# A spectral mixer ahead of routed experts: batch 1 through DRAM, batch 2's stores put off, nested conditions at the end

## The chip, the cores and the metric

The kernel runs on one core of one Trainium2 chip. The metric is the time of one execution on the device in microseconds, as the median of several runs. The core has five engines that run their own instruction streams in order and wait for each other through semaphores: TensorE (PE, with its weight load PEld), VectorE (DVE), ScalarE (ACT), GpSimd (POOL) and SyncE (SP). SP, ACT and POOL also issue DMAs; all DMAs share 16 DMA engines.

## The reference, cut to what matters

```python
# x: (8, 2496, 256); filt_r, filt_i: (1249, 256)
X = np.fft.rfft(x, axis=1)
y = np.fft.irfft(X * (filt_r + 1j * filt_i)[None], n=2496, axis=1)   # (8, 2496, 256)

x = y.reshape(19968, 256)
expert_idx = token_ids * np.int64(2654435761) % np.int64(8)
for e in range(8):
    mask = expert_idx == e
    h = np.maximum(x[mask] @ w1[e], 0.0)         # w1[e]: (256, 1024)
    out[mask] = h @ w2[e]                        # w2[e]: (1024, 256)
```

Each of the 8 batches is filtered along its 2496 positions by a Fourier transform. Then each of the 19968 rows goes through the two-layer network of the one expert that its token number names.

## The kernel before, in words

**The transform.** 2496 = 39 x 64, so a transform has three stages. Stage 1 multiplies by the 39-point table `wf_t`. Stage 2 multiplies by the 64-point table `d_t` (`forward`, PSUM tile `pb`), applies the filter on VectorE (four products and a sum, tiles `y` and `z`), and multiplies by `e_t` (`back`, tile `pc`). Stage 3 multiplies by `wi_t` (tile `pd`) and scatters the finished rows into the DRAM tensor `xs`, each row at the place that its expert gives it (`scatter`, an indirect DMA on GpSimd, 22 for each batch). Stage 1 and stage 3 of a batch come as 6 groups u = 0 to 5 (`NU`), stage 2 as 10 pairs of frequencies (`NS // 2`).

**Two ways between the stages.** Batches 2 to 7 go through DRAM. `stage1` writes rows into the buffer `t1`, which is stored to the DRAM tile `d1` (three parts v = 0 to 2, four DMAs). `load2` reads `d1` back in another order, as five groups g of four frequencies (tile `t2`, two DMAs each). `back` stores its result to `d2`, and `load4` reads that for stage 3 (tile `t`, parts v). Batches 0 and 1 stay on the chip: `stage1_c` writes columns into `mixed`, `turn2` transposes them on TensorE (tile `pt`), `back_c` and `turn4` do the same on the way to stage 3. The buffers `t1`, `t2`, `g`, `mixed` and `out` of the batches are all parts of one tile `mid` of ten slots, or of the space of the expert weights `wts`; `slots` says which.

**The experts.** Rows are taken in tiles of 128 that belong to one expert each. `load` fetches the rows of a pair of tiles (`xg`; the first four loads in `begin`, half of them on ScalarE's queue), `numbers` copies their row numbers (`no`), `turn` transposes a tile (`xt`), `up` does the first layer (32 matmuls, `ups`), `down` the second (16 matmuls, `dps`) and scatters the result into the output. `weights` loads an expert's weights where the expert changes. Tiles come in four groups (`STAGES`): the first 30 tiles hold rows of batches 0 and 1 alone, so they can run while later batches are still transformed. 159 tiles (`NSURE`) are always there; up to four more depend on the token numbers, and each of three conditions (`tc.If`) runs one, one or two of them.

**The order of the work** is written out by hand: the list `todo` holds pairs of a time and a piece of work and is sorted. Pieces with a negative time come ahead of the first tile. A time from 0 on is counted in tiles: a piece at 5.0 to 5.5 stands ahead of tile 5's up, one at 5.5 to 6.0 between its up and its down. `spaced(t0, t1, n)` spreads n pieces evenly. `chain(k)` interleaves `turn2` of step k + 1, `back_c` of step k - 2 and `forward` of step k over batches 0 and 1, so steps 10 to 19 belong to batch 1. `part1`, `part2` and `part3` are stages 1 to 3 of the later batches with their loads. Each engine and each queue carries out its instructions in this order, so a wait holds up all that stands behind it on the same engine.

Of the kernel before, what the change touches and what calls it, by code (L numbers as in the profile page):

```python
# [20 lines left out]
B, S, C = 8, 2496, 256  # L21
# [8 lines left out]
NS, NQ = N1 // 2 + 1, 64  # L30
# [3 lines left out]
NK = 2 * H * NS  # L34
SG = 4
XG = 4
NU = (HN + XG) // XG
# [6 lines left out]
NT = (N + E * (TB - 1)) // TB  # L44
# [8 lines left out]
NSURE = NT - 4  # L53
# [66 lines left out]
def kernel(  # L120
# [10 lines left out]
    nc = tc.nc  # L131
# [9 lines left out]
    def pool(stack, name, bufs, space=None):  # L141
# [28 lines left out]
    mid = cpool.tile([P, 10, SG * C], F32)  # L170
    wts = cpool.tile([P, 4, DP * F], F32)
    held = wts[:].rearrange("p k f -> p (k f)")
    slots = {"t1": [mid[0:NK, k:k + 2, :].rearrange("p k (j c) -> p (k j) c", c=C) for k in (5, 7)],
             "t2": [mid[:, k, :].rearrange("p (s c) -> p s c", c=C) for k in range(4)],
             "g": [mid[:, k, :].rearrange("p (s c) -> p s c", c=C) for k in (9, 4)]}

    def slot(kind):
        slots[kind].append(slots[kind].pop(0))
        return slots[kind][-1]

    class Batch:


        def __init__(self, b):
            self.b = b
            self.d1 = self.d2 = None
            self.x, self.t2, self.t4, self.p = {}, {}, {}, {}
            self.g = None
            if b < 2:

                own = mid[:, 5 * b:5 * b + 5, :].rearrange("p k f -> p (k f)")
                self.mixed = own.rearrange("p (h n s) -> p h n s", h=2, s=NS)
                after = (held[:, 0:NS * C] if b == 0 else mid[:, 0:5, :].rearrange("p k f -> p (k f)"))
                self.out = after.rearrange("p (h n s) -> p h n s", h=2, s=NS)

        def load1(self, v):
# [42 lines left out]
        def stage1(self, u):  # L239
            if self.d1 is None:  # L240
                self.d1 = dpool.tile([N2, 2 * NS, C], F32, name=f"d1_{self.b}", tag="d1")
            v, half = divmod(u, XL // XG)
            sl = slice(half * XG, half * XG + XG)
            if half == 0:
                self.t1 = slot("t1")
            self.products(wf_t, (NR, NR), 2 * NS, self.x[v][:, sl, :], self.t1[:, sl, :], nc.scalar.copy, u, "pa")
            if half == 1:


                eng = nc.scalar if self.b == 2 else nc.gpsimd  # L250
                for dram, chip in self.parts(self.d1, self.t1, v):
                    eng.dma_start(out=dram, in_=chip)

        def load2(self, g):
            t2 = slot("t2")
            for p in range(2):
                a0 = p * NS + SG * g
                nc.sync.dma_start(out=t2[p:P:2, :, :],
                                  in_=self.d1[:, a0:a0 + SG, :])
            self.t2[g] = t2  # L260

        def forward(self, u):
            ps = fps.tile([P, 2, C], F32, name=f"pb_{self.b}_{u}", tag="f")
            for i in range(2):
                s = 2 * u + i
                rhs = self.t2[u][:, i, :] if self.b < 2 else self.t2[s // SG][:, s % SG, :]
                nc.tensor.matmul(out=ps[:, i, :], lhsT=d_t[:, s, :], rhs=rhs, start=True, stop=True)  # L267

            sl = slice(2 * u, 2 * u + 2)
            y, z = [ppool.tile([P, 2, C], F32, name=f"{n}_{self.b}_{u}", tag="p") for n in "yz"]
            nc.vector.tensor_tensor(out=y[:], in0=ps[:], in1=f_t[0][:, sl, :], op=OP.mult)  # L273
            for k in range(2):
                a, b = slice(64 * k, 64 * k + 64), slice(64 - 64 * k, 128 - 64 * k)
                nc.vector.tensor_tensor(out=z[b], in0=ps[a], in1=f_t[1][a, sl, :], op=OP.mult)  # L276
            nc.vector.tensor_tensor(out=y[:], in0=y[:], in1=z[:], op=OP.add)  # L277
            self.p[u] = y
# [119 lines left out]
    def weights(i, which):  # L398

        if i >= NT:  # L400
            return
        if i >= 2 and which == 0:
            ws[i] = ws[i - 2][0:2]
        eng, kw = nc.sync, {}
        if which == 0:
            ws[i].append(eng.value_load(chunk_i[0:1, 0, i:i + 1], min_val=0, max_val=E - 1))
            if i >= 2:
                ws[i].append(eng.value_load(chunk_i[0:1, 1, i:i + 1], min_val=0, max_val=1))
        e = ws[i][2]
        if i >= 2:  # L410
            kw = {"cond": ws[i][3]}
        if which == 0:


            for f in (slice(0, F // 2), slice(F // 2, F)) if i < 2 else (slice(0, F),):
                eng.dma_start(out=ws[i][0][:, :, f],
                              in_=moe_w1[bass.ds(e, 1)].rearrange("one (p dp) f -> p (one dp) f", p=P)[:, :, f], **kw)
        else:
            eng.dma_start(out=ws[i][1], in_=moe_w2[bass.ds(e, 1)].rearrange("one (fp p) d -> p (one fp) d", p=P), **kw)
# [234 lines left out]
    def spaced(t0, t1, n):  # L654
        return [t0 + (t1 - t0) * u / n for u in range(n)]

    def part1(b, at, loads=None):
        bt = batches[b]
        if loads is None:

            loads = [at[2 * v] - 2.5 * (at[1] - at[0]) for v in range(NV)]
        return ([(at[u], lambda u=u: bt.stage1(u)) for u in range(NU)] +
                [(loads[v], lambda v=v: bt.load1(v)) for v in range(NV) if b > 0])

    def part2(b, at, ready):
        if isinstance(ready, list):
            bt = batches[b]
            return ([(at[u], lambda u=u: bt.stage2(u)) for u in range(NS // 2 + 1)] +
                    [(t, lambda g=g: bt.load2(g)) for g, t in enumerate(ready)])
        bt = batches[b]  # L670
        return ([(at[u], lambda u=u: bt.stage2(u)) for u in range(NS // 2 + 1)] +
                [(max(at[2 * g] - 4.5 * (at[1] - at[0]), ready), lambda g=g: bt.load2(g)) for g in range(NS // SG)])

    def part3(b, at, ready=None):
        bt = batches[b]
        if b < 2:
            return [(at[u], lambda u=u: bt.stage3(u)) for u in range(NU)]
        return ([(at[u], lambda u=u: bt.stage3(u)) for u in range(NU)] +
                [(max(at[2 * v] - 2.5 * (at[1] - at[0]), ready), lambda v=v: bt.load4(v)) for v in range(NV)])
# [5 lines left out]

    def chain(k):

        for step, j in ((Batch.turn2, k + 1), (Batch.back_c, k - 2), (Batch.forward, k)):
            if 0 <= j < NS:
                step(batches[j // (NS // 2)], j % (NS // 2))  # L690


# [6 lines left out]
    todo += [(t, lambda k=k: way_back(k)) for k, t in enumerate((-150.44, -146.5, -141.8, -137.5, -133.8))]  # L699
    todo += [(-150.4, lambda: first.turn2(0))]  # L700
    todo += [(t, lambda k=k: chain(k)) for k, t in enumerate(spaced(-150, -105, NS + 2))]
    todo += [(t, lambda u=u: second.stage1_c(u)) for u, t in enumerate(spaced(-147.5, -132, NU))]
    for bt, at in ((first, spaced(-123.7, -105, NU)), (second, spaced(-103, -85, NU))):
        todo += [(t - 2.6, lambda bt=bt, u=u: bt.turn4(u)) for u, t in enumerate(at)]
        todo += [(t, lambda bt=bt, u=u: bt.stage3(u)) for u, t in enumerate(at)]
    todo += [(-135, lambda: nc.sync.dma_start(out=wi_t[:], in_=wi_dram.ap()))]
    todo += part1(2, spaced(-102, -87, NU), [-119, -117.5, -116])
    todo += [(t, lambda k=k: weights(k // 2, k % 2)) for k, t in enumerate((-99, -98.9, -98.8, -98.7))]
    todo += [(-76, lambda: begin())]

    todo += part1(3, spaced(1.5, 6.5, NU), [-74.6, -74.5, 2.5]) + part1(4, spaced(15, 20.5, NU))
    todo += part1(5, spaced(21, 27, NU)) + part1(6, spaced(36, 46, NU)) + part1(7, spaced(50, 60, NU))
    todo += part2(2, [-74] + spaced(.55, 5.5, N_2 - 1), [-78, -75, -74.9, -74.8, 1.2]) + part2(3, spaced(9.2, 15.7, N_2), 6.6)
    todo += part2(4, spaced(22, 31, N_2), 20.5) + part2(5, spaced(31.2, 46, N_2), 28)
    todo += part2(6, spaced(48, 62, N_2), 47) + part2(7, spaced(63.2, 80, N_2), 61)
    todo += part3(2, spaced(7, 14, NU), 5.6) + part3(3, spaced(17, 25, NU), 15.6)
    todo += part3(4, spaced(33, 44, NU), 31.5) + part3(5, spaced(49, 63, NU), 46.5)
    todo += part3(6, spaced(67, 83, NU), 62) + part3(7, spaced(84, 101, NU), 81)
    todo.sort(key=lambda t: t[0])
# [95 lines left out]
    used = []  # L815
# [23 lines left out]
    spare = mid[:, 0, :].rearrange("p (i d t) -> p i d t", i=NT - NSURE, d=DP)  # L839
    for i in range(NSURE, NT):  # L840
        turn(i, spare[:, i - NSURE])
    for some in (range(NSURE, NSURE + 1), range(NSURE + 1, NSURE + 2), range(NSURE + 2, NT)):
        with tc.If(used[0] > some[0]):
            for i in some:
                ht = work.tile([P, FP, TB], F32, name=f"ht_{i}", tag="ht")
                numbers(i)
                up(i, ht)
                weights(i + 2, 0)
                down(i, ht)
                weights(i + 2, 1)  # L850


# [1 line left out]
_INS = ['x', 'filt_r', 'filt_i', 'moe_token_ids', 'moe_w1', 'moe_w2']  # L854
# [24 lines left out]
```

## Time and profile before

| what | value |
|---|---|
| median of 9 runs | 1520.94 us (1517.33 to 1523.45) |
| the profiled execution's own time | 1523.25 us |
| its span, first to last instruction | 1521.4 us |
| mean granted TensorE clock | 0.983 |
| PE, PEld busy | 1456.7 us (96%), 1341.1 us (88%) |
| DVE, ACT, POOL busy | 534.5, 234.0, 499.1 us |
| chain that ended last | PE 88%, DMA 8%, issue 1%, DVE 1% |
| DMA | 226.06 MB, mean 149 GB/s |

In a line of the timeline stand the start in us, the duration in us, the engine, the line of the kernel, the operation, what it writes and reads, and in square brackets how long the engine had been idle and what ended that. SPq, ACTq and POOLq are the queues of these engines: the instructions that issue DMAs, wait, or branch. In a line of the chain stand the start, the duration, and the work or the DMA that took that time. In a line of stretches stand the stretch, its length, the busy time of PE, PEld, DVE, ACT and POOL (with the number of instructions), the granted TensorE clock, the busy share of the DMA engines, and GB/s.

### The profile page before, as it was taken

How to read it: one execution, taken by the hardware profiler on the slowest of the kernel's cores; microseconds unless marked ns; L12 is line 12 of the kernel's file. 1: busy time of each engine (PE TensorE's matmuls, PEld its weight loads, DVE VectorE, ACT ScalarE, POOL GpSimd, SP SyncE). 2: the span in 40 equal slices, each digit the busy share in tenths (PEclk: the TensorE clock that was granted, in tenths of full speed). 3: DMA queues.
4: the chain of work that ended last, by engine and by line, in shares of the span. 5: the costliest groups of instructions: out<-in, count | busy, mean ns of one | idle time of the engine just before them, and what ended most of it. 6: DMA issues, size and time to landing. Idle time of an engine off the chain costs nothing.

```text
span 1521.4 us, 25837 instructions
## 1 busy us (share of the span) xinstructions
PE 1456.7 (96%) x9340; PEld 1341.1 (88%) x9340; DVE 534.5 (35%) x1008; ACT 234.0 (15%) x401; POOL 499.1 (33%) x802
## 2 busy tenths in 40 slices
PE   6995998998999999999999999999999999999996
PEld 6984897897989999989999999899999999999995
DVE  5962533632344443244434442222222221222221
ACT  3652120121121111111111110000000000000000
POOL 6565123544432343224432433233212111211111
PEclk9998999999999999999999999999999999999998
DMA  8267757669855963755657533653422423232320
GB/s 214 69 200 208 237 158 180 210 188 249 255 183 163 256 181 93 226 168 164 193 133 199 177 120 98 176 153 97 134 60 61 129 87 97 52 108 62 92 88 25
DMA packets 186988, 226.06 MB, mean 149 GB/s; under 512 B 101653, under 2 KB 157389, under 8 KB 180890
## 3 DMA queue, kind: packets, MB, share of 16 engines
q1 hardware_dynamic: 154615, 146.92, 35.3%
q0 software_dynamic: 28096, 73.51, 15.0%
q10 hardware_dynamic: 4147, 3.94, 0.9%
q8 instruction: 76, 1.25, 0.3%
q14 instruction: 54, 0.44, 0.1%
HBM read 415.94 MB, written 75.08 MB: 323 GB/s over the span
## 4 chain that ended last, share of the span: by engine, by line
PE 88%; DMA 8%; issue 1%; DVE 1%; POOL 0%; SPq 0%; ACT 0%; ACTq 0%; POOLq 0%; DVEq 0%
PE ups L790 36%; PE dps L802 34%; PE pd L226 5%; PE pb L267 4%; PE pc L289 3%; PE pa L226 3%; DMA t<-d 1%; DMA wts<-in_moe_w_dram 1%; DMA wts<-in_x_dram 1%; DMA d<-mid 1%; PE pc L339 1%; DMA mid<-d 1%; DMA d_t<-d_tbl 1%; PE pu L354 1%; DMA x<-in_x_dram 1%
## 5 line engine op out<-in xcount | busy, mean ns | idle before, releaser
L790 PEld LDWEIGHTS ups<-xt,wts 128*128 128x128 f32 x5088 | 597.4, 193 | 15.9 <-issue 7.5
L790 PE MATMUL ups<-xt,wts 128*128 128x128 f32 x5088 | 598.6, 277 | 4.8 <-issue 3.3
L802 PE MATMUL dps<-wts,ht 128*128 128x256 f32 x2544 | 575.7, 380 | 0.0
L802 PEld LDWEIGHTS dps<-wts,ht 128*128 128x128 f32 x2544 | 475.5, 191 | 60.4 <-ACT mid L292 0.8
L806 POOL DMA_INDIRECT out_dram<-osb,no x159 | 158.3, 995 | 571.4 <-DVE osb L805 456.8
L796 DVE TENSOR_SCALAR ht<-ups 128x512 f32<-128x512 f32 x159 | 110.0, 692 | 490.2 <-PE ups L790 484.1
L794 ACT ACTIVATE ht<-ups 128x512 f32<-128x512 f32 x159 | 94.9, 597 | 880.3 <-PE ups L790 835.0
L385 POOL DMA_INDIRECT xs<-o,sidx x176 | 178.0, 1011 | 109.5 <-issue 43.3
L805 DVE COPY osb<-dps 128x256 f32<-128x256 f32 x159 | 67.5, 425 | 362.3 <-PE dps L802 360.8
L773 POOL COPY no<-xg 32x2 int32<-32x2 int32 (+1 forms) x328 | 60.2, 184 | 262.3 <-DMA out_dram<-osb,no 180.6
L276 DVE TENSOR_TENSOR z<-pb,filt 64x512 f32<-64x512 f32 x160 | 110.1, 688 | 2.3
L226 PE MATMUL pd<-t,wi_t 120*117 120x256 f32 x320 | 79.8, 394 | 10.4 <-DMA t<-d 10.0
L267 PE MATMUL pb<-mid,d_t 128*128 128x256 f32 x240 | 63.9, 390 | 19.2 <-DMA mid<-d 19.2
L226 PEld LDWEIGHTS pd<-t,wi_t 120*117 120x117 f32 x320 | 58.8, 188 | 23.3 <-DMA t<-d 6.3
L273 DVE TENSOR_TENSOR y<-pb,filt 128x512 f32<-128x512 f32 x80 | 54.3, 679 | 61.6 <-PE pb L267 61.3
L292 ACT COPY mid<-pc 128x512 f32<-128x512 f32 x60 | 35.1, 585 | 230.4 <-PE pc L289 230.4
L780 DVE STREAM_TRANSPOSE xt<-xg 128x256 f32<-128x256 f32 x159 | 69.1, 434 | 0.0
L267 PEld LDWEIGHTS pb<-mid,d_t 128*128 128x128 f32 x240 | 44.4, 195 | 25.5 <-issue 16.6
L289 PE MATMUL pc<-y,e_t 128*128 128x256 f32 x240 | 61.7, 380 | 0.0
L277 DVE TENSOR_TENSOR y<-y,z 128x512 f32<-128x512 f32 x80 | 57.9, 723 | 2.7
L226 PE MATMUL pa<-x,wf_t 117*120 117x256 f32 x224 | 53.0, 379 | 0.0
L289 PEld LDWEIGHTS pc<-y,e_t 128*128 128x128 f32 x240 | 45.5, 190 | 6.4 <-issue 0.4
(123 smaller groups left out, 552.7 us busy)
## 6 DMA issues: line engine op xcount, KB each, us to landing
wts<-in_moe_w_dram SPq DMA_DIRECT2D x320, 1024.0 KB
mid<-d SPq DMA_DIRECT2D x60, 256.0 KB
d<-mid POOLq DMA_DIRECT2D x60, 256.0 KB, 4.3
xg<-xs SPq DMA_DIRECT2D x235, 64.0 KB
t<-d SPq DMA_DIRECT2D x12, 960.0 KB
x<-in_x_dram SPq DMA_DIRECT2D x36, 312.0 KB
d<-mid POOLq DMA_DIRECT2D x10, 960.0 KB, 8.8
xg<-xs SPq DMA_DIRECT2D x77, 65.0 KB
```

What stands on the lines that cost most here:

```text
L226: nc.tensor.matmul(out=ps[0:cols * H, k, :], lhsT=w[:], rhs=src[:, 2 * i + k, :], start=True, stop=True)
L267: nc.tensor.matmul(out=ps[:, i, :], lhsT=d_t[:, s, :], rhs=rhs, start=True, stop=True)
L276: nc.vector.tensor_tensor(out=z[b], in0=ps[a], in1=f_t[1][a, sl, :], op=OP.mult)
L289: nc.tensor.matmul(out=ps[:, i, :], lhsT=e_t[:, 2 * u + i, :], rhs=pr[:, i, :], start=True, stop=True)
L385: st = nc.gpsimd.indirect_dma_start(out=xs[:], out_offset=bass.IndirectOffsetOnAxis(ap=index, axis=0), in_=rows, in_offset=None, bounds_ch ...
L780: nc.vector.transpose(out=xt[i].rearrange("p d (a t) -> p a d t", t=32), in_=xg[i][0][:, 4 * xg[i][1]:4 * xg[i][1] + 4, 0:C // 4].rearrang ...
L790: nc.tensor.matmul(out=ps[:, k, :], lhsT=w1[:, dp, fp * P:(fp + 1) * P], rhs=xt[i][:, dp, :], start=(dp == 0), stop=(dp == DP - 1))
L794: nc.scalar.activation(out=dst, in_=ps[:], func=AF.Relu)
L796: nc.vector.tensor_scalar_max(dst, ps[:], 0.0)
L802: nc.tensor.matmul(out=ps[:, 0, :], lhsT=ht[:, fp, :], rhs=w2[:, fp, :], start=(fp == 0), stop=(fp == FP - 1))
L805: nc.vector.tensor_copy(out=o[:], in_=ps[:, 0, :])
L806: st = nc.gpsimd.indirect_dma_start(out=out[:], out_offset=bass.IndirectOffsetOnAxis(ap=to_rows[i], axis=0), in_=o[:], in_offset=None, bou ...
```

## The change

1. Batch 1 (the second) uses `stage1` in place of `stage1_c`: its rows are stored to `d1` from ScalarE's queue, and five `load2` (from -134 on) read them back; `turn2` remains for batch 0 alone. Behind stage 2 it stays on the chip as before. The slots of `mid` are dealt out anew.
2. Batch 2 (the third): stage 1 of u = 0 and 1 stays between batch 1's stage-3 groups, u = 2 to 5 come behind the last of them (-86 to -84.5). The stores of its parts v = 1 and 2 are kept in `put_off` and issued on ScalarE's queue behind the first loads of `begin`. Its `load2` follow at -75 and later, and its first stage-2 piece moves from -74, ahead of tile 0, to 0.55, behind tile 0's up. The last of its stage 2 moves from 5.005 to 5.505, its stage 3 from 7 to 14 to 8 to 14.5, with the `load4` of v = 1 from 6.42 to 7.46.
3. Stage 1 of batch 6 moves from 36 to 46 to 35 to 44.5.
4. The three conditions at the end are nested: the second stands inside the first, the third inside the second.

```diff
-    slots = {"t1": [mid[0:NK, k:k + 2, :].rearrange("p k (j c) -> p (k j) c", c=C) for k in (5, 7)],
-             "t2": [mid[:, k, :].rearrange("p (s c) -> p s c", c=C) for k in range(4)],
-             "g": [mid[:, k, :].rearrange("p (s c) -> p s c", c=C) for k in (9, 4)]}
+    parts = {"t1": [mid[0:NK, k:k + 2, :].rearrange("p k (j c) -> p (k j) c", c=C) for k in (0, 2, 5, 7)],
+             "s": [mid[:, k, :].rearrange("p (s c) -> p s c", c=C) for k in range(10)]}
+
+    slots = {"t1": parts["t1"][0:2], "t2": parts["s"][5:9], "g": [parts["s"][k] for k in (9, 4)],
+             "t1_1": parts["t1"][2:4], "t2_1": [parts["s"][k] for k in (9, 0, 1, 2, 3)]}
...
+    put_off = []
...
-                own = mid[:, 5 * b:5 * b + 5, :].rearrange("p k f -> p (k f)")
-                self.mixed = own.rearrange("p (h n s) -> p h n s", h=2, s=NS)
-                after = (held[:, 0:NS * C] if b == 0 else mid[:, 0:5, :].rearrange("p k f -> p (k f)"))
+                if b == 0:
+                    self.mixed = mid[:, 0:5, :].rearrange("p k f -> p (k f)").rearrange("p (h n s) -> p h n s", h=2, s=NS)
+                after = (held[:, 0:NS * C] if b == 0 else mid[:, 5:10, :].rearrange("p k f -> p (k f)"))
...
-                self.t1 = slot("t1")
+                self.t1 = slot("t1_1" if self.b == 1 else "t1")
...
-                eng = nc.scalar if self.b == 2 else nc.gpsimd
-                for dram, chip in self.parts(self.d1, self.t1, v):
+                eng = nc.scalar if self.b <= 2 else nc.gpsimd
+                moves = self.parts(self.d1, self.t1, v)
+                if self.b == 2 and v > 0:
+                    put_off.extend(moves)
+                    return
+                for dram, chip in moves:
                     eng.dma_start(out=dram, in_=chip)
...
-        for step, j in ((Batch.turn2, k + 1), (Batch.back_c, k - 2), (Batch.forward, k)):
-            if 0 <= j < NS:
+        for step, j, end in ((Batch.turn2, k + 1, NS // 2), (Batch.back_c, k - 2, NS), (Batch.forward, k, NS)):
+            if 0 <= j < end:
...
-    todo += [(t, lambda u=u: second.stage1_c(u)) for u, t in enumerate(spaced(-147.5, -132, NU))]
+    todo += [(t, lambda u=u: second.stage1(u)) for u, t in enumerate(spaced(-147.5, -132, NU))]
+    todo += [(t, lambda g=g: second.load2(g)) for g, t in enumerate((-134, -133.5, -133.4, -133.3, -133.2))]
...
-    todo += part1(2, spaced(-102, -87, NU), [-119, -117.5, -116])
+    todo += [(t, lambda v=v: batches[2].load1(v)) for v, t in enumerate((-119, -117.5, -116))]
+    todo += [(t, lambda u=u: batches[2].stage1(u)) for u, t in enumerate((-101.5, -99.5, -86, -85.5, -85, -84.5))]
+
+    todo += [(-75.5, lambda: [nc.scalar.dma_start(out=dram, in_=chip) for dram, chip in put_off])]
...
-    todo += part1(5, spaced(21, 27, NU)) + part1(6, spaced(36, 46, NU)) + part1(7, spaced(50, 60, NU))
-    todo += part2(2, [-74] + spaced(.55, 5.5, N_2 - 1), [-78, -75, -74.9, -74.8, 1.2]) + part2(3, spaced(9.2, 15.7, N_2), 6.6)
+    todo += part1(5, spaced(21, 27, NU)) + part1(6, spaced(35, 44.5, NU)) + part1(7, spaced(50, 60, NU))
+    todo += part2(2, spaced(.55, 6, N_2), [-75, -74.9, -74.8, -74.7, 1.2]) + part2(3, spaced(9.2, 15.7, N_2), 6.6)
...
-    todo += part3(2, spaced(7, 14, NU), 5.6) + part3(3, spaced(17, 25, NU), 15.6)
+    todo += part3(2, spaced(8, 14.5, NU), 5.8) + part3(3, spaced(17, 25, NU), 15.6)
...
-    for some in (range(NSURE, NSURE + 1), range(NSURE + 1, NSURE + 2), range(NSURE + 2, NT)):
-        with tc.If(used[0] > some[0]):
-            for i in some:
+    blocks = [range(NSURE, NSURE + 1), range(NSURE + 1, NSURE + 2), range(NSURE + 2, NT)]
+
+    def rest(k):
+        with tc.If(used[0] > blocks[k][0]):
+            for i in blocks[k]:
...
+            if k + 1 < len(blocks):
+                rest(k + 1)
+
+    rest(0)
```

## The prediction

> **What bounds the kernel now.** I read the page first: TensorE (PE) is busy 96% of 1521.4 us and carries 88% of the chain that ended last, so from the first expert tile on a microsecond is gained only where PE stands still or runs at half clock. The busy time in stretches shows where that is:
>
> ```profile
> 120.00:134.00 14.00, 13.22 (x68) 9.90 (x66) 5.38 (x19) 6.65 (x14) 10.64 (x12) 1.00 0.97 296
> 134.00:144.00 10.00, 0.00 (x0) 0.00 (x0) 0.00 (x0) 0.63 (x2) 4.22 (x5) 0.68 0.57 157
> 144.00:155.00 11.00, 2.65 (x7) 1.81 (x8) 3.12 (x5) 0.00 (x0) 0.72 (x4) 0.50 0.86 216
> ...
> 228.00:245.00 17.00, 11.12 (x53) 9.52 (x52) 2.95 (x6) 0.60 (x1) 4.29 (x5) 0.80 0.85 204
> ```
>
> The second column is PE's busy time, the third from the end the granted clock. Between 134 and 155 us PE works 2.65 us, at a clock that falls to 0.50; around 232 it loses 5.9 us. The chain in order of time says for what it waits:
>
> ```profile
> 132.99 10.04 DMA d<-mid
> ...
> 144.14 4.75 DMA mid<-d
> ...
> 149.03 2.04 PE pb L267 x4
> 151.08 3.32 issue
> 154.39 5.58 PE ups L790 x32
> ...
> 227.07 10.59 DMA t<-d
> 237.66 0.04 issue
> 237.70 3.77 PE pd L226 x8
> 241.47 4.57 PE ups L790 x32
> ```
>
> Batch 2 (the third) stores stage 1, reads it back, does one forward step, and only then does the first tile's up start. The timeline shows what else the first tile needs:
>
> ```profile
> 139.60 0.89 POOL L385 DMA_INDIRECT xs<-o,sidx  x1 [0.32 <-issue]
> 143.18 1.44 SPq L258 DMA_DIRECT2D mid<-d  x2
> 143.55 1.89 ACTq L756 DMA_DIRECT2D xg<-xs  x4
> 145.00 2.57 SPq L756 DMA_DIRECT2D xg<-xs  x4
> 147.94 0.85 POOL L773 COPY no<-xg 32x2 int32<-32x2 int32 x4 [7.44 <-DMA xg<-xs]
> ...
> 153.85 0.44 DVE L780 STREAM_TRANSPOSE xt<-xg 128x256 f32<-128x256 f32 x1
> ```
>
> The last scatter of batch 1 lands, the rows are loaded (xg), and the transpose for tile 0 stands on VectorE behind the forward step (its four products run 151.11 to 153.94). Last, the instructions of the line with the conditions, and of the line after them:
>
> ```profile
> L843 POOLq INC_SWDGE_SEM  x3: 1742/1760/1780, 1508.0 to 1512.2; - x3
> L874 POOLq DRAIN  x3: 46/103/6607, 1514.0 to 1521.2; - x3
> ```
>
> PE ends at 1507.3; after it GpSimd works through three skipped conditions (only 159 tiles ran) and a drain of 6.6 us. The profiled execution took 1523.25 us (1.85 outside its span), 2.31 above the median of 1520.94. I sum against 1523.25 and carry the difference to the median.
>
> **End: nested conditions.** Skipping the outer one skips all. The three increments start at 1508.0, some 1510.1 and 1512.2, 2.1 apart with branch and wait; the drain starts when they are through. Two fewer: -4.2, taken as -4.1. Bounds: 0, if the one skip has to make up for each block in turn, or if the drain ends on something else; -4.2. The last output scatter takes no part: it is issued at 1508.03, and SyncE's wait for it, reached at 1514.1, passes at once.
>
> The Trainium skill (Runtime: NRT & Kernel Launch, Instruction fetch mechanics) speaks against this edit: a taken branch beyond the two resident pages of instructions waits for a fetch. The three branches cost GpSimd 45 to 61 ns and PE 219 to 725 ns here, so if the rule bites, it bites on PE, which reaches its last wait at 1508.8, 12 us before GpSimd's drain ends; by the rule the sum would lie nearer to 0 only if GpSimd's longer jump left its pages.
>
> **Tiles 5 to 8: batch 2 half a tile later, its stage 3 from tile 8 instead of 7.** Now, counted from tile 5's up at 216.43, load4 is issued 10.6 us later, lands another 10.6 later, and stage 3's pd starts at 21.3, though PE was through at 15.4: a stall of 5.88 us. PE then runs at half clock: pd 3.77 instead of the 1.73 of such groups elsewhere, up 4.57 instead of 3.57. Together 5.9 + 2.0 + 1.0 = 8.9. After the change the last back step comes behind tile 5's up, and PE has up 3.57, back 0.86, pa 0.98, down 3.46, then up and down of tiles 6 and 7 (14.06): 22.9 us. The store behind the back step is not later: GpSimd was held until 223.17 anyway by the copies of row numbers (L773), which wait for an output scatter. So load4 is still issued at 10.6; even at an unchanged 10.6 it lands 1.7 before its use. It will be quicker, as the second part (load4 of v = 1, now issued 0.9 behind it and sharing the engines) moves from 6.42 to 7.46. I take -8.9; bounds -9.5 and 0 (GpSimd later by over 1.7 us, or the next transfer late instead). What is late next is load4 of batch 3 at 335.73, whose own stall of 4.1 stays. Batch 6's stage 1, a tile earlier at 35 to 44.5, lies in a stretch where PE is never idle: 0.
>
> **Up to 105 us: batch 1 through DRAM.** Stage 1 as rows costs PE the same (8 matmuls in 1.73 against 16 in 1.78), and ScalarE the same copies. Ten turn2 go: 10 x 0.64 = 6.4 us of PE and 10 x 0.59 of ScalarE. Added on ScalarE's queue are four stores (0.32 to 0.36, the last 0.91), behind which its copies for batch 0's chain wait; on SP ten loads ahead of batch 2's x, which is used 40 us later. The chain's step 10 (forward at 66.77 now, VectorE ready for it at 68.55) must wait for the round trip: last copies at 59.6, store issues to 60.9, landing. For that the trace has 5.8 (600 KB from GpSimd's queue) and 10.0 (the same pair at 133 us, with scatters beside it), and a floor of 2.3 (25.6 KB). DMA moved almost nothing at 46 to 60 us, so I take 3; then 5.0 from SP's issue to PE (5.85 at 143.18 to 149.03, with xg beside it). Data at 69, so VectorE starts that step 1.4 late (69.9 instead of 68.55). Bounds: 0 late, and 60.9 + 10.0 + 5.85 = 76.8, 9 late.
>
> Who waits: GpSimd's 44 scatters, from 79.1, one in 1.29 us. They need 56.8 but end at 140.5, 4.6 of it gaps (before 86.72, at 98.27, 111.35, and 135.71). The removed 6.4 us of PE and batch 2's last four stage-1 groups (4 x 1.73), now behind batch 1's rows, close the later gaps; so the end moves from 140.5 to 139.5 (138 to 146).
>
> **133 to 165 us: the first tile.** From the last scatter's end to the load of rows 3.05 us, to the copy of row numbers 4.4, then the transpose at once, since no forward step stands ahead: up(0) at 139.5 + 3.05 + 4.4 + 0.5 = 147.4 instead of 154.39, ending at 153.0 (5.58, half clock again: PE is idle from some 138). But forward(0) of batch 2 stands right behind it, and its data now come late. The three put-off stores (1600 KB) follow the four xg issues on ScalarE, from 144.4; 2.3 to start, 5.5 at the 296 GB/s of 120 to 134, and about 1 for xg beside them: landed at 153. SP's load2 takes 5.5 to 5.85: forward(0) at 158.5. At half clock 1.75, then down(0) 3.46 + 1.3: done at 165.0. It ends at 165.15 now, with one forward and one back (1.73) done that then remain. Net +1.6; as batch 1's store may well be quicker than taken, I use +1. Bounds: forward(0) 1 us behind an up(0) that ends at 151.5 (scatters at 138), at full clock, gives some -6; stores as slow as GpSimd's (8.8 and 5.8 one after the other) give 165 and +8. SP stands behind load2's wait until 153 with x of batch 3 (used at 170 now), xg of tile 4 and weights behind it: 5 us of loads, in time.
>
> The clock has its own row: 0.50 from 137.6 on, and back 3.7 us after PE resumes at 154.39. The Trainium skill (TensorE: Matmul & The Clock Gate, Part 1: The HAM clock gate) lets it return after one busy window of 3.4 us. By that figure a stall costs 1.7 on top, the one at 232 so 7.6 where its rows give 8.9; the rows decide.
>
> **Sum.** -4.1 - 8.9 + 1 = -12.0: 1511.25 for the profiled execution, 1508.9 for the median: **1509 us**.
>
> **Rivals.** (a) The round trips hide better than taken (front -6): 1520.9 - 19 = 1502. For it: the DMA engines are idle at 46 to 60 us. (b) The end pays nothing: 1513. For it: four blocks' scatters still have to be made up for on four semaphores; against it: the third condition made up for two with one increment. (c) The stall at 232 stays in another coat (PE waits for the next load): -4.1 + 1, 1518. (d) Slower: batch 2's round trip, now begun only behind the load of rows, becomes the bound. At the worst rows (11.3 from store to release at 118.89 to 130.21, 10.0 for the last pair, 11.56 for a read at 335.73) forward(0) waits until 144.4 + 21.3 + 11.6 = 177.3, 18.8 beyond my 158.5: front +20, 1528. It decides once forward(0) comes after some 173.5. Against it: at 144 the scatters that slowed those stores are over.
>
> **How the numbers follow.** 0.2% is 3.0 us, about what a measurement of this kernel tells from no change. Forecast 0.61 (1505 to 1513), (a) 0.10, (b) 0.13, (c) 0.09, (d) 0.07. (c) lies at the border, half of it counted as no change. Faster 0.61 + 0.10 + 0.13 + 0.04 = 0.88; same 0.05; slower 0.07. The range takes in (a) to (c): 1502 to 1518; (d) is left out.
>
> **What would show it.** Up(0) near 147 with PE idle between it and a forward step at 156 to 160; no wait for t at pd of batch 2; one INC_SWDGE_SEM and a drain starting near PE's end + 2.7; 10 x 4 transposes of turn2 gone, and 5.2 MB more moved. I am wrong if the scatters end after 142, if forward(0) comes after 165, or if the drain starts no earlier behind PE's end.

## The result, and the profile after

The changed kernel takes 1516.25 us, the median of 11 runs (1512.88 to 1518.92), against 1520.79 for the kernel before: 4.5 us less, a ratio of 0.9968 with a 95% interval from 0.9959 to 0.9977. The direction was foretold, and the time lies in the range; the gain is little more than a third of the 12 us of the sum.

The profiled execution took 1516.1 us, with a span of 1514.4. The busy time in stretches, in the first fence of the changed kernel, in the second of the kernel before (second column the length, third TensorE's busy time, the third from the end its granted clock):

```profile
61.50:70.80 9.30, 0.06 (x2) 0.04 (x1) 2.18 (x4) 0.83 (x2) 2.40 (x4) 0.75 0.57 144
70.80:76.40 5.60, 5.60 (x22) 5.22 (x23) 1.00 (x2) 1.28 (x2) 0.00 (x0) 0.50 0.50 157
...
232.00:250.00 18.00, 18.00 (x115) 16.71 (x115) 3.12 (x7) 1.83 (x4) 5.36 (x10) 1.00 0.85 200
```

```profile
61.50:70.80 9.30, 8.04 (x52) 7.01 (x51) 8.99 (x14) 3.83 (x6) 2.08 (x3) 1.00 0.10 15
```

The last row of the first fence is the gain: around 232 us TensorE is never idle now, at the full clock. Its first row is the loss, at a place that the prediction gave 1.4 us: TensorE does nothing from 61.5 to 70.8, where the kernel before works 8.04 of 9.30 us, and the 5.6 us behind it run at half clock. All that follows is late: the first of the 44 scatters of batches 0 and 1 starts at 91.6 instead of 79.1, the last at 149.8 instead of 139.6.

What TensorE waited for, in the changed kernel (total, times, longest):

```profile
PE ups L802 <- DVE xt L792: 12.3, 1, 12.3
PE pt L336 <- DMA mid<-d: 9.2, 1, 9.2
...
PE pb L275 <- DMA mid<-d: 6.8, 2, 5.0
...
PE pd L230 <- DMA t<-d: 4.1, 1, 4.1
```

The second line is new: pt is the transpose of turn2, which reads `mid` as stage 1 of batch 0 left it and needs no transfer. The timeline of the changed kernel shows who holds it:

```profile
61.42 0.81 ACTq L260 DMA_DIRECT2D d<-mid  x2
...
66.39 9.91 SPq L266 DMA_DIRECT2D mid<-d  x9
70.80 1.14 PE L336 MATMUL pt<-ident,mid 128*128 128x128 f32 x4 [9.24 <-DMA mid<-d]
```

The last stores of batch 1's stage 1 go out behind 61.42, SyncE's reads start at 66.39, and the moment the first read has landed (70.7), turn2(9) of batch 0 runs. turn2(9) reads slots 0 to 4 of `mid`; load2(0) of batch 1 writes slot 9. But load2(0) is emitted at -134 and the chain's step 8, which holds turn2(9), at -133.6. The reading that the experiments test: the build orders the later instruction behind the earlier write into the same buffer, though into another slot. The rest of step 8 and step 9, batch 0's own work, stand in TensorE's queue behind it.

The first tile's up, and the end:

```profile
149.81 0.90 POOL L393 DMA_INDIRECT xs<-o,sidx  x1 [0.30 <-issue]
152.11 1.83 SPq L768 DMA_DIRECT2D xg<-xs  x4
154.73 3.11 ACTq L719 DMA_DIRECT2D d<-mid  x3
156.30 6.40 PE L802 MATMUL ups<-xt,wts 128*128 128x128 f32 x32 [12.27 <-DVE xt L792]
163.60 4.98 SPq L266 DMA_DIRECT2D mid<-d  x8
167.66 2.04 PE L275 MATMUL pb<-mid,d_t 128*128 128x256 f32 x4 [4.96 <-DMA mid<-d]
```

Up(0) follows the last scatter in 6.5 us, where it took 14.8 before; the put-off stores go out at 154.73, and forward(0) waits for their way through DRAM, 4.96 us of TensorE. The ups of tiles 6 and 8, in the first fence of the changed kernel, in the second of the kernel before:

```profile
235.56 3.73 PE L802 MATMUL ups<-xt,wts 128*128 128x128 f32 x32
...
251.34 3.74 PE L802 MATMUL ups<-xt,wts 128*128 128x128 f32 x32
```

```profile
224.64 3.73 PE L790 MATMUL ups<-xt,wts 128*128 128x128 f32 x32
...
251.06 3.74 PE L790 MATMUL ups<-xt,wts 128*128 128x128 f32 x32
```

The changed kernel is 10.9 us behind at tile 6 and 0.3 at tile 8, on the other side of the stall that is gone. Of the end, the line with the condition and the last line of the program, both in the changed kernel:

```profile
L857 PEldq COMPARE_BRANCH  x1: 380/380/380, 1501.5 to 1501.5; - x1
...
L857 POOLq COMPARE_BRANCH  x1: 61/61/61, 1504.6 to 1504.6; - x1
L857 POOLq INC_SWDGE_SEM  x1: 1802/1802/1802, 1505.1 to 1505.1; - x1
```

```profile
L891 POOLq DRAIN  x3: 46/103/6607, 1506.9 to 1514.1; - x3
```

One increment instead of three; the drain of 6.6 us starts at 1506.9, 2.8 behind TensorE's end (1504.1), where it started 6.7 behind it before. That is 3.9 us.

### The profile page after: what moved, and what is told of

Same layout as the page of the kernel before. It is cut to its first block, busy times and chain, and to the rows that moved or that the text cites. A ratio compares the mean times of both kernels' runs of the same rounds, so it can differ in the third digit from the quotient of the medians.

```text
span 1514.4 us, 25664 instructions
## 1 busy us (share of the span) xinstructions
PE 1449.9 (96%) x9256; PEld 1329.4 (88%) x9256; DVE 537.6 (35%) x1008; ACT 228.8 (15%) x391; POOL 500.1 (33%) x802
## 3 DMA queue, kind: packets, MB, share of 16 engines
q1 hardware_dynamic: 155415, 149.54, 35.9%
## 4 chain that ended last, share of the span: by engine, by line
PE 88%; DMA 6%; DVE 2%; issue 1%; POOL 1%; SPq 0%; ACT 0%; ACTq 0%; POOLq 0%; DVEq 0%
PE ups L802 36%; PE dps L814 35%; PE pd L230 4%; PE pb L275 4%; PE pc L297 3%; PE pa L230 3%; DMA wts<-in_x_dram 1%; DMA d<-mid 1%; DMA mid<-d 1%; PE pc L347 1%; DVE z L284 1%; POOL xs L393 1%; DMA d_t<-d_tbl 1%; DMA t<-d 1%; DMA xg<-xs 1%
## 5 line engine op out<-in xcount | busy, mean ns | idle before, releaser
L275 PE MATMUL pb<-mid,d_t 128*128 128x256 f32 x280 | 73.2, 384 | 6.8 <-DMA mid<-d 6.8
L300 ACT COPY mid<-pc 128x512 f32<-128x512 f32 x60 | 35.2, 586 | 233.3 <-PE pc L297 232.2
L275 PEld LDWEIGHTS pb<-mid,d_t 128*128 128x128 f32 x280 | 50.6, 192 | 13.1 <-issue 5.5
L230 PE MATMUL pa<-x,wf_t 117*120 117x256 f32 x248 | 58.7, 380 | 1.2 <-DVE z L284 1.2
L232 ACT COPY mid<-pa 120x512 f32<-120x512 f32 x70 | 40.9, 586 | 98.7 <-PE pa L230 98.7
```

The lines of the kernel that those rows point to most:

```text
L230: nc.tensor.matmul(out=ps[0:cols * H, k, :], lhsT=w[:], rhs=src[:, 2 * i + k, :], start=True, stop=True)
```

## The experiments

The runs went in five sets, each on one chip and with the kernel before beside it: 1520.96 us in the first set and 1520.20 in the fourth, but 1533.49, 1531.18 and 1533.06 in the second, third and fifth, on two other chips (the third and the fifth on the same one). A kernel is compared only with the kernel before of its own set; what those two chips do differently is told further down.

**Is turn2(9)'s wait the loss?** First the reads are moved behind step 8 of the chain (set 1):

```diff
-    todo += [(t, lambda g=g: second.load2(g)) for g, t in enumerate((-134, -133.5, -133.4, -133.3, -133.2))]
+    todo += [(t, lambda g=g: second.load2(g)) for g, t in enumerate((-133.6, -133.5, -133.4, -133.3, -133.2))]
```

> The changed kernel with one number different: batch 1's first load2 stands at -133.6, just behind step 8 of the chain (-133.64), instead of at -134, just ahead of it. Theory W (a false wait: turn2 of batch 0's last pair, in step 8, waits for the load of batch 1 into a slot that it does not read, so steps 8 and 9 stand still with step 10): that transpose no longer waits near 62 us; the wait moves to forward of step 10, whose data come at about 70.8 as now, so VectorE starts it about 3 us later than in the kernel before (68.55) instead of 12.5. First scatter at 82 to 84 instead of 91.6, first up at 147 to 149 instead of 156.3, the whole 8 to 10 us below the changed kernel: 1506 to 1508. Rival R (the round trip through DRAM is what costs; whoever waits, the chain stops for it): PE stands still as long a few instructions later, first scatter still at 88 or later, at most 3 us gained: 1513 to 1516.

Measured: 1511.15 us, 0.9929 of the kernel before (0.9907 to 0.9952). No wait at turn2(9); step 10's forward waits 1.72 us for the read. The first scatter starts at 79.0, the last at 138.1, up(0) at 144.5. One emission time, changed by 0.4, is worth 5.1 us. The time lies between the two expectations; the scatters, no later than W foretold, speak for W, though 2.7 us of their place are this execution's early start (its chain's third forward at 34.2, against 36.9 in the kernel before and 37.2 in the changed kernel). Up(6) starts at 223.8, 11.8 ahead of the changed kernel, but TensorE ends only 5.9 ahead of it: the short waits far behind the front (3.37 us near 641, 1.57 near 954) are 1.82 and none in the profile of the changed kernel.

Then the reads keep their place, and only the first one's target is put into another buffer, so that turn2(9) has nothing in common with it:

```diff
+    ... "t2_1": [held[:, NS * C + 4 * C:NS * C + 8 * C].rearrange("p (s c) -> p s c", c=C)] + [parts["s"][k] for k in (0, 1, 2, 3)]
-    ... "t2_1": [parts["s"][k] for k in (9, 0, 1, 2, 3)]
```

> The changed kernel, its loads at their places in the order, but the first read of batch 1 (load2(0)) goes into a free part of another buffer instead of slot 9 of mid. In the built program turn2(9) of batch 0 then has no wait for a DMA. Theory W (in the changed kernel turn2(9) stood 9.24 us for a read that it doesn't need, only because both touch mid): no wait of TensorE at turn2(9), some 1 to 3 us of a wait at step 10's forward, first scatter at 78 to 81, last at 137 to 140, up(0) at 143 to 146, time 1509 to 1512, as with the load placed behind that step (1511.15). Rival R (the round trip itself is the price, and TensorE stands as long at step 10 instead): first scatter at 87 or later, time 1514 to 1517.

> The changed kernel with the first read of batch 1 in a part of another buffer, as before, now beside the others of this set. Theory W (turn2(9) waited for nothing it needs): no wait of TensorE at turn2(9), one of 1 to 3 us at step 10's forward, up(0) 9 to 13 us earlier than in the changed kernel, time 4 to 8 below it. Rival R (the round trip has the same price anyway): time within 2 us of the changed kernel.

> The changed kernel with the first read of batch 1 in another buffer. Where answers are prompt, theory W (the 9.24 us at turn2(9) were a wait for nothing): 8 to 11 below the kernel before, no wait at turn2(9), up(0) at 143 to 146. Rival R (the way through DRAM has this price whoever waits): 3 to 6 below. Where answers come late: 1 below to 3 above, as twice before.

Set 4: 1510.88 us, 0.9934 (0.9911 to 0.9958), 9.3 below the kernel before. The timeline of this run has turn2(9) at once, and the wait where the prediction had placed it, at step 10's forward:

```profile
62.10 0.80 PE L336 MATMUL pt<-ident,mid 128*128 128x128 f32 x4
62.12 0.81 ACTq L260 DMA_DIRECT2D d<-mid  x2
...
66.93 1.16 SPq L266 DMA_DIRECT2D wts<-d  x2
...
71.25 2.05 PE L275 MATMUL pb<-wts,d_t 128*128 128x256 f32 x4 [2.46 <-DMA wts<-d]
```

The round trip costs TensorE 2.46 us here, not 9.24. The difference, 6.8, is what up(6) gains (228.8 against 235.6); between the two medians lie 5.4. One miss: up(0) came at 149.3, not at 143 to 146. The chain's third forward starts with that of the kernel before (37.0 against 36.9), its eighth at 59.7 against 56.9, so 2.7 us are lost ahead of the round trip. TensorE waits there for VectorE's products (1.39 and 1.20 us, the second at batch 1's stage 1, which as rows takes its PSUM buffers from the same set as the forward steps; that this is the reason was not tried). The changed kernel has a wait of 1.19 at the same place. In sets 2 and 3 the same kernel gave 0.9988 (0.9971 to 1.0005) and 1.001 (0.999 to 1.003), 6 to 7 us below the changed kernel of those sets: the same step as on the other chips. No wait at turn2(9) was there either, and step 10's forward waited 2.66 and 2.75 us.

The other side of the test, batch 1 through DRAM as the only edit (set 2):

> The kernel before with only batch 1 sent through DRAM (stage 1 as rows, ten reads, ten turn2 fewer), with the reads' places of the changed kernel; conditions, batch 2's stages and stage 3 as before. Theory W (this part alone carries the front's loss): first scatter at 90 to 93, last at 149 to 152, up(0) at 164 to 167, the stalls behind as before: 1528 to 1533. Rival R (a good part of the loss came from batch 2's stores put off, or shows only together with them): up(0) at 155 to 159, 1519 to 1525.

Measured: 1541.70 against 1533.49, a ratio of 1.0056 (1.0038 to 1.0075). W's 7 to 12 us above the kernel before are met (8.2), and so is its up(0), at 166.5; its absolute times were written for the other chip. Its scatters are not: they run from 87.5 to 156.9, the first earlier in an execution whose chain started 2.9 us ahead of the first profile of the kernel before, the last later with 13.8 us of gaps between them (see the late chips below). TensorE's wait is there without any of the other edits:

```profile
PE pt L330 <- DMA mid<-d: 8.9, 1, 8.9
```

**What do the other parts give?** All of the change but batch 1's way through DRAM (the slots, `stage1_c` and `turn2` as before):

> All of the change except its first part: batch 1 stays on the chip with the slots of before; batch 2's stage 1 behind batch 1's rows, the stores put off, the later stage 2 and 3 and the nested conditions are in. By the sum of the prediction (end -3.8 as measured, stall at tile 7 -8.9, first tile near 146 to 148 with forward of batch 2 some 11 us behind its start, worth 0 to +2): 1508 to 1511, first scatter at 79 as before. Under W and under R alike this is better than the changed kernel by 5 to 8 us; if it is no better than 1515, neither holds and the loss lies in batch 2's part.

> All of the change but batch 1 through DRAM, once more beside the changed kernel on one chip. Where batch 1's way through DRAM gains nothing even without its wait: 0 to 3 us below the kernel with the read in its own place, 6 to 9 below the changed kernel, 10 to 13 below the kernel before. If that way does pay once the wait is gone: 2 or more above the kernel with the read in its own place.

Set 1: 1509.05 us, 0.9918 (0.9896 to 0.9940), 11.9 below the kernel before, what the prediction had given the whole change. Batch 1 through DRAM therefore gains nothing even without its wait: 1511.15 and 1510.88 with it, 1509.05 without. In set 3: 0.997 (0.995 to 0.999), 10.7 below the changed kernel, 4.7 below the one with its own buffer and 2.3 below the kernel before. All three lie outside what was expected (6 to 9, 0 to 3, 10 to 13); the chip is one of the two treated below.

The nested conditions alone, and stage 3 of batch 2 a tile later alone (both set 1):

```diff
-    todo += part3(2, spaced(7, 14, NU), 5.6) + part3(3, spaced(17, 25, NU), 15.6)
+    todo += part3(2, spaced(8, 14.5, NU), 5.8) + part3(3, spaced(17, 25, NU), 15.6)
```

> The kernel before with the nested conditions alone. From the two profiles the drain should start 2.8 us after PE's end instead of 6.7, and the time fall by 3.8: 1517. If the drain waits for something else: no change.

> The kernel before with batch 2's stage 3 at 8 to 14.5 (loads from 5.8) alone; its stage 2 stays. The stall of 5.9 us ahead of pd and the half clock behind it (3.0) go: -8 to -9, 1512 to 1513. If the wait only moves to the next load (batch 3's at 336 us, or rows of a tile), less than -4.

Conditions: 1515.36, 0.9966 (0.9951 to 0.9981). Stage 3: 1512.4, 0.993 (0.9905 to 0.9954), the wait at 232 gone. The intervals, some -2.9 to -7.5 and -7.0 to -14.4 us, hold the terms -4.1 and -8.9 of the sum.

Batch 2's part of the front alone (set 4):

```diff
-    todo += part1(2, spaced(-102, -87, NU), [-119, -117.5, -116])
+    todo += [(t, lambda v=v: batches[2].load1(v)) for v, t in enumerate((-119, -117.5, -116))]
+    todo += [(t, lambda u=u: batches[2].stage1(u)) for u, t in enumerate((-101.5, -99.5, -86, -85.5, -85, -84.5))]
+    todo += [(-75.5, lambda: [nc.scalar.dma_start(out=dram, in_=chip) for dram, chip in put_off])]
...
-    ... part2(2, [-74] + spaced(.55, 5.5, N_2 - 1), [-78, -75, -74.9, -74.8, 1.2])
+    ... part2(2, spaced(.55, 6, N_2), [-75, -74.9, -74.8, -74.7, 1.2])
```

> The kernel before with only batch 2's part of the front: four groups of stage 1 behind batch 1's last rows, the stores put off, the steps behind up(0), batch 6's stage 1 a tile earlier. From the runs with batch 1 on the chip (-11.9) less the nested conditions (-5.4) and stage 3 (-8.5), where answers are prompt: theory P (up(0) comes 9 us earlier, and it is given back ahead of forward(0) and in the steps that remain): 0 to +3 against the kernel before, up(0) near 145, 5 us of wait ahead of forward(0). Rival Q (it gains 3 or more). Where answers come late (kernel before near 1532): +6 to +11 by P, since scatters issued without gaps hold the answers longer.

Measured: 1518.69, 0.9982 (0.9968 to 0.9995): 1.5 us gained, just outside P's 0 to +3 and short of Q's 3. The wait ahead of forward(0) is there (4.38); up(0) came at 149.4, not near 145, half of it because the chain started 2.2 us later than in the first profile of the kernel before. Part of the 1.5 is not the front's: the wait ahead of stage 3 (near 232 in the first profile) is 4.14 us in this run, against 5.88 in the first profile of the kernel before and 7.17 in the one of the same set; here the last back step comes half a tile later and stage 3 isn't moved. The three parts by themselves come to 5.6 + 8.6 + 1.5 = 15.7, together to 11.9; this stall, shortened by 1.7 to 3.0 us in one of them and removed in another, is counted twice and accounts for about half or more of the 3.8.

**The two chips that answer late.** The changed kernel, once more in sets 2 and 3, and the kernel before, profiled in set 4:

> The changed kernel once more, beside the others on the same chip. In its first profile TensorE's wait near 650 us was 1.82 (3.49 before, 2.5 to 3.4 in four variants) and the one near 963 us was missing (1.50 before, 1.6 to 1.9 in the variants). Theory C (that was chance in that execution): waits of 2.5 to 3.5 and 1.5 to 1.9 again, a profiled span of 1516 to 1519, and a median of 1515 to 1518. Rival S (a late front takes these waits away for good): 1.8 and none again, span 1513 to 1515.

> The changed kernel once more as the mark for this set: 4 to 5 us below the kernel before where engines answer TensorE at once, as in the first comparison; at or above it where the trace shows them answering some microseconds late, as on the chip of the second set. The wait of TensorE near 70 us (turn2(9)) 8.5 to 9.5 in either.

> The kernel before, for its profile beside the others of this set. Theory A (on some chips an engine's answer to TensorE comes microseconds late while GpSimd issues transfers one after the other; on the chip of the first profiles it doesn't): where the times are near 1521 no answer of VectorE behind up comes over 0.5 us late, up(0) at 153 to 156; where they are near 1532, up to 5 us late, up(0) at 158 to 166. Rival B (other transfers are slower on those chips, GpSimd has no part): near 1532 without late answers behind up.

In set 2 the changed kernel took 1539.01 (1.0023, 1.0010 to 1.0037), in set 3 1539.6 (1.0049, 1.0029 to 1.0069): on these chips it is slower than the kernel before. The wait at turn2(9) was 9.18 and 8.96. New are waits with the releaser "remote": the record that should have ended them lies microseconds back. The timeline of set 3's run:

```profile
352.24 1.06 PE L802 MATMUL ups<-xt,wts 128*128 128x128 f32 x8
...
354.08 0.97 POOL L393 DMA_INDIRECT xs<-blank,at_i  x1 [0.30 <-issue]
...
355.36 0.97 POOL L818 DMA_INDIRECT out_dram<-osb,no  x1 [0.30 <-issue]
356.32 1.14 POOL L304 DMA_DIRECT2D d<-mid  x2
...
358.00 1.07 ACT L232 COPY mid<-pa 120x512 f32<-120x512 f32 x2 [5.16 <-remote]
358.01 0.69 DVE L808 TENSOR_SCALAR ht<-ups 128x512 f32<-128x512 f32 x1 [10.42 <-remote]
```

Up's matmuls end at 353.3; VectorE, which waits for nothing else, starts on them at 358.0, ScalarE at the same moment, just behind a row of five GpSimd transfers. Over all 159 tiles VectorE starts 0.10 us behind up in the median on every chip; the longest is 0.46 us in ten profiles from prompt chips and 4.67 to 4.75 in the ten from these two. The instructions themselves take the same time on both, and so do the transfers' packets: the 155415 of the largest queue took 35.9% of the changed kernel's 1514.4 us in the first profile, and 35.2 and 34.6% of 1542.3 here, which speaks against rival B, slower transfers. In the front it hits the scatters: in the changed kernel the gaps between the 44 add up to 2.5 us in the first profile and to 14.3 and 14.4 in sets 2 and 3, and the last one starts at 162 instead of 150. The kernel before, in the fourth set, answered promptly (at most 0.45) and took 1520.16, so A's first half holds, but for up(0) at 151.5, not at 153 to 156; its second half wasn't met with, since the kernel before was not profiled on such a chip. That GpSimd's transfers cause the lateness is argued from where it falls; no run changed them. It falls there plainly: in the ten late profiles VectorE starts over 0.5 us behind up in 142 of the 314 tiles where GpSimd was issuing a transfer within 0.4 us of up's end, and in 24 of the other 1276; on the prompt chips in none. And the question that the second set was to settle, whether the first profile's short late waits (1.82 at 650 us, none at 963) were chance, could not be answered on these chips; in the four profiles of set 4 these waits vary between 1.3 and 2.9 and between 0.9 and 1.8.

**Can the 5 us ahead of forward(0) be had back?** Batch 1 stays on the chip, and batch 2's steps begin a tile later; then also with batch 3's x ahead of the put-off reads on SyncE:

```diff
-    part2(2, spaced(.55, 6, N_2), [-75, -74.9, -74.8, -74.7, 1.2])
+    part2(2, spaced(1.55, 6, N_2), [-75, -74.9, -74.8, -74.7, 2.1])
...
-    part1(3, spaced(1.5, 6.5, NU), [-74.6, -74.5, 2.5])
+    part1(3, spaced(1.5, 6.5, NU), [-75.2, -75.1, 2.5])
```

> As the kernel with batch 1 kept on the chip and all the rest of the change (1509.05), but batch 2's forward and back steps begin one tile later (behind up of tile 1 instead of tile 0; the last still before load4), so that TensorE has down(0) and up(1) to do while the put-off stores and their reads run. In that kernel's profile TensorE stood still for 5.05 us ahead of forward(0) and worked at half clock behind it (forward and down(0) some 2 us longer). Theory T (the put-off round trip is bare only because forward(0) stands directly behind up(0)): the 5.05 go and 1 to 2 of the half clock with them, no new wait comes behind: 1502 to 1504. Rival R (the steps, now closer together, bring the wait for t near 232 back, 3 to 6 us): 1506 to 1509.

> Batch 1 kept on the chip, all the rest of the change, batch 2's forward and back steps one tile later, and now also the first two parts of batch 3's x loaded ahead of the reads of batch 2's put-off stores (in the run before this one they stood behind those reads on SyncE's queue, and TensorE waited 8.79 us for them ahead of batch 3's stage 1). Theory T: the wait ahead of forward(0) (5 us in the kernel with batch 1 on the chip) and its half clock go, and no wait for x comes: 5 to 8 us below that kernel, 16 to 19 below the kernel before. Rival R (TensorE then waits for the reads at forward(0) all the same, or for x): 0 to 3 us below that kernel.

> The kernel with batch 1 on the chip, batch 2's steps a tile later and batch 3's x ahead of the put-off reads, once more. Theory T where answers are prompt: no wait ahead of forward(0), none for x, 15 to 19 below the kernel before. Rival R: 10 to 13 below it, as without the later steps. Where answers come late: 2 to 5 below it, as in the first run of this kernel.

The first edit alone (set 2) gave 1538.15, 1.0035 (1.0019 to 1.0050): a miss for both expectations: the chip was a late one, and TensorE then waited 8.79 us for x of batch 3, which stands on SyncE behind the reads. With x moved ahead: 0.9976 (0.9961 to 0.9991) in set 3 and, in set 4, 1508.52, 0.9929 (0.9905 to 0.9954). Rival R: no better than with the early steps. The timeline of set 4's run says why:

```profile
163.13 1.97 PE L273 MATMUL pb<-mid,d_t 128*128 128x256 f32 x8 [1.88 <-DMA mid<-d]
...
167.24 1.10 PE L295 MATMUL pc<-y,e_t 128*128 128x256 f32 x4 [2.14 <-DVE y L283]
...
194.94 1.13 PE L295 MATMUL pc<-y,e_t 128*128 128x256 f32 x4 [1.32 <-DVE y L283]
```

The 5 us are gone and 5.3 are back: 1.88 for the reads, now behind x, and 2.14 and 1.32 where eleven steps in 4.5 tiles put two forward steps into one half tile, so that only one forward step (and at the second place a back step) stands between a forward step and the back step that needs its products. Spaced evenly, half a tile apart (set 5), the first variant from behind down(0), with batch 3's x where it was and its stage 1 half a tile later, the second from behind up(1), with the x ahead of the reads:

```diff
-    part2(2, spaced(.55, 6, N_2), [-75, -74.9, -74.8, -74.7, 1.2])  ...  part3(2, spaced(8, 14.5, NU), 5.8)
+    part2(2, spaced(1.05, 6.55, N_2), [-75, -74.9, -74.8, -74.7, 1.6])  ...  part3(2, spaced(8.5, 14.5, NU), 6.1)
...
+    part2(2, spaced(1.55, 7.05, N_2), [-75, -74.9, -74.8, -74.7, 2.1])  ...  part3(2, spaced(9, 14.5, NU), 6.6)
```

> Batch 1 on the chip, all the rest of the change, and batch 2's forward and back steps from behind down(0) on (half a tile later than in the change), evenly half a tile apart, its stage 3 half a tile later too, batch 3's stage 1 half a tile later. Theory T (the wait ahead of forward(0) goes once it has work ahead of it and its steps don't crowd): a wait of 0 to 1.5 us there instead of 5, none of 2 us at the back steps behind it: 13 to 17 below the kernel before, 3 to 5 below the kernel with the steps crowded (1508.52 against 1520.2). Rival R (what is saved there returns as a wait elsewhere ahead of tile 8): 10 to 12.5 below the kernel before. Where answers to TensorE come late: 3 to 8 below it.

> The kernel with the steps behind up(1) and batch 3's x ahead of the put-off reads, its steps now evenly half a tile apart and stage 3 a tile later. In the crowded form TensorE waited 1.88 us ahead of forward(0), 2.14 at the first back step and 1.32 at a later one. Theory T: the first stays, the other two go: 13.5 to 16 below the kernel before. Rival R: 10 to 12.5 below it. Where answers come late: 3 to 8 below it.

Measured: 1522.21, 0.9921 (0.9900 to 0.9942), and 1522.49, 0.9927 (0.9904 to 0.9951), 10.9 and 10.6 below the kernel before, more than the 3 to 8 expected where answers come late; the same chip had given 0.997 without and 0.9976 with the crowded steps. For T: the waits at the back steps are gone. Against it, a wait ahead of forward(0) stays, 2.64 in the first variant, where 0 to 1.5 was expected, and 2.08 in the second. On this chip the two are the best kernels that were run, and noise doesn't tell them apart; on a prompt chip they weren't tried, and there the kernels with batch 1 on the chip (1509.05, 1508.52) are the best.

## Why the prediction was right and wrong

- **End, -4.1: right.** 3.9 in the profile, by the step named: one increment (1802 ns), the drain 2.8 behind TensorE's end where 2.7 was foretold. Of the fetch that was weighed there nothing is seen: the longer jump took GpSimd 61 ns and TensorE 380.
- **Tiles 5 to 8, -8.9: right.** Counted at the starts of up, the changed kernel is 10.9 us behind the kernel before at tile 6, 1.3 at tile 7 and 0.3 at tile 8, so 9.6 by the step over the stall and 10.6 in all. Of these 1.73 are no gain: at tile 8 the changed kernel has done one group of stage 3, the kernel before two. That leaves 8.9. Late next, as said, was load4 of batch 3, with 4.08 us.
- **Forward(0) of batch 2: right.** 11.1 us behind up(0)'s start foretold (158.5 - 147.4), 11.4 measured.
- **Front, +1: this is the step that failed.** Measured +10.9 at tile 6. The round trip was well sized (data at 69 foretold, 70.7 measured), and so was its use ("VectorE starts that step 1.4 late"; 1.72 and 2.46 of TensorE in the two prompt-chip runs without the other wait). What was missed is one of those who wait: the prediction named only the chain's step 10, which reads the data, and behind it the scatters. Step 8's turn2 waited too, emitted behind the read and touching the same buffer: its forward starts 12.9 later than before (73.4 against 60.5), of which 9.24 are this wait, 2.1 were already lost at the step ahead of it (59.0 against 56.9, the waits for VectorE, priced at nothing), and the rest lies in the half clock behind the wait. So the scatters began 12.5 late instead of 1.4. With the read in its own buffer (set 4) up(6) comes 6.7 us earlier, so the wait and its half clock carry 6.7 of the 9.9 that were missed; the 2.7 us lost there ahead of the round trip are most of the rest. Once begun, they closed their gaps as said: the 44 take 58.2 from first to last start instead of 60.5.
- **The ten turn2 and their ScalarE copies, 6.4 us of TensorE less:** removed as counted, and worth nothing on the path: without batch 1's way through DRAM the first scatter starts at 78.8 and the last at 138.4; with it, and without the wait at turn2(9), at 83.9 and 142.8 (79.0 and 138.1 in the execution that started early).
- **The wrong-side test** the prediction set itself, scatters ending after 142 and forward(0) after 165, came true at 150.7 and 167.7, and pointed at the right term. Of the rivals none was it: (d) had a late forward(0), but by batch 2's round trip, which behaved.
- **From +9.9 in the front to +7.5 in the median.** In the profile the miss is smaller still, 4.9 (7.15 gained): TensorE, 2.0 behind at tile 8 with the group that it owes, ends 3.2 ahead. These 5.2 us lie in late waits that were shorter in this one profile: 1.82 near 649 us instead of 3.48 and no half clock behind it, none near 963 instead of 1.50. The profile of before was taken 2.3 above its median, so some of this is chance; how much is the change's, the runs don't settle.
- **The clock.** The 9.24 us cost more than themselves: TensorE resumes at 70.80, the clock is back at 76.40, 5.6 later. The Trainium skill (TensorE: Matmul & The Clock Gate, Part 1: The HAM clock gate) lets the clock return after at least one busy window of about 3.4 us. The 5.6 here and the 3.7 at 154.39 both lie above one window, so the price that the prediction worked out from just one was too low for both rows.

## What to carry to other kernels

When a transfer is moved to an earlier place in the order, ask not only who reads its data, but which instructions emitted behind it touch the same buffer at all: they may be made to wait for it, and an in-order queue passes the wait to work that has nothing to do with it. Place the transfer behind the last such instruction, or give it a buffer of its own. A stall that two edits would remove is gained only once, and a step that is moved past a transfer needs work between itself and the step that feeds it, or the wait just changes its name.

## What the runs showed of the hardware

Two of the chips let engines start up to 4.75 us behind the matmul that they waited for (at most 0.46 on the others), while instructions took the same time; the medians of the kernel before are 10 to 13 us longer there, and the change that is worth 4.5 us on one chip costs 5.5 and 8.4 on these two. That the late answers are the whole of this difference is not shown. A gain of a third of a per cent is a statement about a chip as well as about a kernel.
